# Transposing the exponentials of q with VectorE in 32x32 blocks, from q loaded twice

## The chip, the cores and the metric

The kernel runs on one core of a Trainium2 chip. Time is what one execution takes on the device, in microseconds (us). The core has engines that run beside each other and wait for one another through semaphores: PE (TensorE, the matrix products; PEld is its weight load), DVE (VectorE), ACT (ScalarE), POOL (GpSimd) and SP, which here only issues transfers. Sixteen DMA engines carry out the transfers. SBUF is the on-chip memory with 128 partitions; PSUM holds the results of PE.

## The reference, cut to what matters

The first part is an attention without a score matrix, for 8 batches of 8 heads with 576 tokens of 64 elements. k is normalized over the tokens, q over the 64 elements of a token:

```python
q_s = np.exp(q - np.max(q, axis=-1, keepdims=True))
q_s = q_s / (np.sum(q_s, axis=-1, keepdims=True) + 1e-09)
k_s = np.exp(k - np.max(k, axis=2, keepdims=True))
k_s = k_s / (np.sum(k_s, axis=2, keepdims=True) + 1e-09)
kv = np.einsum('bhsd,bhse->bhde', k_s, v)
x = np.einsum('bhsd,bhde->bhse', q_s, kv)
```

The heads are put side by side, so that a token has 512 elements. The second part picks, in each batch, the 128 tokens of the highest score `x @ w_gate`, runs them through a two-layer network (512 to 1024 with a ReLU, and back) and adds the result times a sigmoid of the score; all other tokens stay as they are:

```python
h = np.maximum(xe @ w1, 0.0)
ye = h @ w2
out[b, top_idx] = x[b, top_idx] + g[:, None] * ye
```

## The kernel before

The attention is cut into 16 units, each of one batch and four heads. Two heads share a tile's 128 partitions, a second pair lies beside it. A unit loads k, v and q (0.59 MB each) into one of three buffers for each of them, so unit u uses buffer u % 3. ACT takes the exponentials of k (`k_exp`) and of q (`q_exp`) and copies v with a column of ones (`v_copy`). PE forms kv for the four heads (`kv_mm`), VectorE normalizes it (`kv_out`), and PE multiplies the exponentials of q with it (`x_mm`), with a column of ones for the sum and one for the score. VectorE divides by the sum (`x_sums`, `x_scale`), and the result is stored (`x_store`).

A matrix product on PE sums over partitions, so q must lie with its 64 elements on partitions. q is loaded with tokens on partitions: a partition of a pair of heads has nine tokens in a row. `q_t` turns it: 18 transposes on PE for a unit (L349, a product with an identity) into PSUM in two parts, of five and of four rows, and a copy of each part back into SBUF. From unit 5 on ACT makes the copy of the first part (L356) and VectorE that of the second (L354); units 0 to 2 use larger transposes (L342).

The dense network of a batch runs two units behind and longer, in pieces that are woven in between: `mlp1` (L544) in odd stages, `mlp2` (L554) in even ones. A stage s of the main loop (L746) holds the attention products of unit s, kv of unit s + 1, the exponentials of q of unit s + 1 and of k of unit s + 2, and one layer of a batch. In odd stages a batch is complete: `score` and `rows` form its row of scores, five compares on VectorE (`ranks`, L446) count for each token how many are above it, and `hits` (L463) marks the ranks. In the next stage `search` finds the tokens' numbers on PE (L473), and POOL gathers the rows (L487). `turn` (L524, copied by L532) transposes the gathered rows for the next layer.

The order of all instructions is written out by hand; every engine runs its own in that order. Transfers of q, k and v and the stores are issued by SP in the order of `queues`: store of unit s (L405), then k and v (L141), then q (L135) of unit s + 3; the first of these loads waits for the last product of `x_mm(s)`. q is loaded in two transfers, of five and of four rows, each over all 128 partitions. A store is two transfers of 64 partitions. k and v are two transfers each of every second partition.

The three q buffers have 18 rows of 64 elements. `ones_f` (for some products at the start), `order_minus_p` (read by L258) and the tiles `hit_f` and `far` (used for batch 0 alone, L499 to L504) are tiles of their own.

Of the kernel before, what the change touches and what calls it, by code (L numbers as in the profile page):

```python
# [8 lines left out]
F32 = mybir.dt.float32  # L9
BF16 = mybir.dt.bfloat16  # L10
I32 = mybir.dt.int32
AF = mybir.ActivationFunctionType
# [5 lines left out]
def kernel(  # L18
# [23 lines left out]
    nc = tc.nc  # L42
    B, H, S, D = q.shape
    DM, F = moe_w1.shape
    P = 128
    R = 5
    N2 = R - 1
    T = R + N2
    RP = N2 * P + P // 2
# [3 lines left out]
    SD = S * D  # L53
# [18 lines left out]
    const = ctx.enter_context(tc.tile_pool(name="const", bufs=1))  # L72
    ld = ctx.enter_context(tc.tile_pool(name="ld", bufs=3))
    at = ctx.enter_context(tc.tile_pool(name="at", bufs=2))
    xp = ctx.enter_context(tc.tile_pool(name="xp", bufs=2))
    md = ctx.enter_context(tc.tile_pool(name="md", bufs=2))
# [3 lines left out]
    def bank(tag, bufs):  # L80
        return ps.tile([P, 512], F32, tag=tag, name=tag, bufs=bufs)

    def pair(tag, bufs=1):
        return ps.tile([P, 2, 512], F32, tag=tag, name=tag, bufs=bufs)
# [4 lines left out]
    def part(i):  # L89
        return slice(64 * i, 64 * i + 64)  # L90
# [7 lines left out]
    NU = len(units)  # L98
# [2 lines left out]

    LD = 3
    FLAT = 0, 1
    RR = 4 * R
    raw = {w: [const.tile([P, 2 * T if w == "q" else RR, D], F32, name=f"{w}{n}") for n in range(LD)] for w in "qkv"}

    def view(t, paired):
        return t.rearrange("p (h r) d -> p h r d", h=4) if paired else t[:, :2 * T].rearrange("p (i r) d -> p i r d", i=2)
# [6 lines left out]
    def load(u, which, after=None, split=False, flat=False):  # L115
        b, qd = units[u]
        for what in which:
            src = {"q": q, "k": k, "v": v}[what]
            first = src[place(b), 4 * qd].offset
            dmas = []  # L120
            if flat:
                t = view(raw[what][u % LD], False)
                if split:
                    for h, queue in enumerate((nc.scalar, nc.sync)):
                        dmas.append(queue.dma_start(out=t[:, h].rearrange("p r d -> p (r d)"),
                                                    in_=bass.AP(tensor=src.tensor, offset=first + 2 * h * SD,
                                                                ap=[[T * D, P], [1, T * D]])))
                else:
                    dmas.append(nc.sync.dma_start(out=t.rearrange("p i r d -> p i (r d)"),  # L129
                                                  in_=bass.AP(tensor=src.tensor, offset=first,  # L130
                                                              ap=[[T * D, P], [2 * SD, 2], [1, T * D]])))
            elif what == "q":
                t = view(raw[what][u % LD], False)
                for r0, r1 in ROWS:
                    dmas.append(nc.sync.dma_start(out=t[:, :, r0:r1].rearrange("p i r d -> p i (r d)"),  # L135
                                                  in_=bass.AP(tensor=src.tensor, offset=first + r0 * D,
                                                              ap=[[T * D, P], [2 * SD, 2], [1, (r1 - r0) * D]])))
            else:
                t = view(raw[what][u % LD], True)
                for n, rows in ((1, N2), (0, R)):  # L140
                    dmas.append(nc.sync.dma_start(out=t[n::2, :, :rows].rearrange("p h r d -> p h (r d)"),  # L141
                                                  in_=bass.AP(tensor=src.tensor, offset=first + n * R * D,
                                                              ap=[[T * D, 64], [SD, 4], [1, rows * D]])))
            if after is not None:
                behind(dmas[0], after)
                after = None
        return dmas[-1]

    ROWS = (0, R), (R, T)
    ctx.enter_context(tc.manual_schedule())  # L150
    load(0, "k", split=True, flat=True)
    load(0, "vq", flat=True)

    def clear(u):
        for what in "kv":
# [5 lines left out]
                                               ap=[[DM, 1], [1, DM]]))  # L161
# [18 lines left out]
    ones_b = const.tile([P, 4 * P], BF16, name="ones_b")  # L180
    nc.vector.memset(ones_b, 1.0)
    w_ps = bank("mm", 2)
    ones_f = const.tile([P, 4 * P], F32, name="ones_f")
    nc.gpsimd.memset(ones_f, 1.0)
    for n in range(WARM):
        nc.tensor.matmul(out=w_ps, lhsT=ones_f[:, :P], rhs=ones_f, start=True, stop=True)
# [20 lines left out]
    for n in range(2):  # L207
        t = const.tile([P, RR, D + 1], F32, name=f"v_ones{n}")
        nc.vector.memset(t[:, :, D:], 1.0)
        v_ones.append(t)  # L210
        t = const.tile([P, 2, C], F32, name=f"kv_w{n}")
        nc.vector.memset(t[:, :, D:D + 1], 1.0)
        kv_w.append(t)
    qrec = const.tile([P, NU, 2, G], F32, name="qrec")
    krec = const.tile([P, NU, 2], F32, name="krec")


    order_minus_p = const.tile([P, RP], F32, name="order_minus_p")
    nc.gpsimd.iota(order_minus_p, pattern=[[1, RP]], base=0, channel_multiplier=-1,
                   allow_small_or_imprecise_dtypes=True)  # L220

# [39 lines left out]
    st = {}  # L261
# [9 lines left out]
    def q_exp(u, c):  # L271
        if c == 0:
            st["qe", u] = at.tile([P, T, 2, D], F32, tag="qe", name="qe")
        r0, r1 = ROWS[c]
        qr = raw["q"][u % LD].rearrange("p (i r) d -> p r i d", i=2)
        nc.scalar.activation(out=st["qe", u][:, r0:r1], in_=qr[:, r0:r1], func=AF.Exp)  # L276

    def v_copy(u, engine=nc.scalar):
# [44 lines left out]
        nc.vector.reduce_sum(out=kw[:, :, D + 1], in_=prod, axis=AX.X)  # L323


    copies = []

    def q_t(u, c, on_vector=False, wide=False, later=False):
# [29 lines left out]
    def x_mm(u, a, wide=False, tag="x"):  # L358

        qT = st["qT", u] if a == 0 else st.pop(("qT", u))  # L360
        x = pair(tag, 2 if tag == "x" else 1)
        kw = kv_w[u % 2]
        for r in range(R):
            for i, c in QUARTERS:
                to = x[part(c), i, r * C:(r + 1) * C]
                if r == N2 and c:
                    last = nc.tensor.matmul(out=to, lhsT=ones_b[part(i), :D], rhs=ones_b[part(i), :C], start=True, stop=True)
                    continue
                if wide and r < N2:
                    if c == 0:  # L370
                        nc.tensor.matmul(out=x[:, i, r * C:(r + 1) * C],
                                         lhsT=qT[part(i), a, r].rearrange("p c t -> p (c t)"), rhs=kw[part(i), a],
                                         start=True, stop=True)
                    continue
                nc.tensor.matmul(out=to, lhsT=qT[part(i), a, r, c], rhs=kw[part(i), a], start=True, stop=True)  # L375
        st["x", u, a] = x[:, :, :R * C].rearrange("p i (r c) -> p i r c", r=R)
        return last

# [113 lines left out]
    def select(b, n, r):  # L492

        k0, m = slots[n]
        if r == 0:
            st["select", n] = bank("mm", 2), md.tile([P, R, P], F32, tag="hit_f", name="hit_f", bufs=1)
        t_ps, hit = st["select", n]
        far = md.tile([P, P], F32, tag="far", name="far")
        nc.scalar.activation(out=far[:, :m], in_=slot_no[:, k0:k0 + m], func=AF.Abs, scale=-1.0,  # L499
                             bias=st["rank", b][:, r:r + 1])  # L500
        nc.scalar.activation(out=hit[:, r, :m], in_=far[:, :m], func=AF.Relu, scale=-1.0, bias=1.0)
        row = xs[b][:, r].rearrange("p n i a d -> p (n i a d)")
        for d in range(KD):
            nc.tensor.matmul(out=t_ps[:, d * m:(d + 1) * m], lhsT=row[:, d * P:(d + 1) * P], rhs=hit[:, r, :m],  # L504
                             start=(r == 0 and d == 0), stop=(r == N2 and d == KD - 1), skip_group_check=True)
        if r == N2:
            turned(b, n, t_ps)
# [74 lines left out]
    def each(step, b, *args):  # L582
        for n in range(n_sl):
            step(b, n, *args)
# [93 lines left out]
    for h in range(2):  # L678
        nc.tensor.matmul(out=g_ps[part(h), :4 * D], lhsT=ones_f[:1, :D],
                         rhs=w_row.rearrange("o (n i x) -> o i n x", i=2, x=2 * D)[:, h], start=True, stop=True)  # L680
# [61 lines left out]
    LAG = 3  # L742
# [3 lines left out]
    for s in range(LAG, NU + LAG):  # L746
# [5 lines left out]
        def pieces(n, to=None):  # L752
            nonlocal f_next
            for _ in range(n if to is None else max(0, to - f_next)):
                each(piece, mlp_b, f_next)
                f_next += 1

        here, follows = s < NU, s + 1 < NU
        ends = s // 2 if here and s % 2 == 1 else None
# [18 lines left out]
        def rows():  # L778
            score_row(ends)

        def ranks(n0=0, n1=R):
            for r in range(n0, n1):
                compare(ends, r)
# [46 lines left out]
        else:  # L830
            if chosen is not None and s not in AFTER:
                pieces(1 if here else 2)
                search()
            if here:
                q_t(s, 0)
                q_t(s, 1, on_vector=s > LAG + 1)
            if follows:
                kv_mm(s + 1)
                kv_out(s + 1)
# [21 lines left out]
            pieces(0, to=2 if follows else 3)  # L861
            if ends is not None:
                rows()
                ranks()
            if s + 2 < NU:
                k_exp(s + 2)
            pieces(0, to=4)
# [4 lines left out]
                number = count_good(good)  # L872
            if ends is not None:
                each(hits, ends)
            pieces(0, to=KF - 1)
            if second and mlp_b + 1 < B:
                each(turn, mlp_b + 1)
# [35 lines left out]
```

## Time and profile before

| | before |
|---|---|
| median of 3 runs | 209.22 us (207.98 to 209.74) |
| time of the profiled execution | 210.15 us |
| its span | 208.4 us |
| transposes of q, units 3 to 15, PE (L349) | 234 in 10.0 us busy |
| copies of them, ACT (L356, 128x640) | 15, mean 692 ns |
| copies of them, DVE (L354, 128x512) | 11, mean 692 ns |
| exponentials of q, ACT (L276) | 32 in 20.1 us busy |
| compares, DVE (L446) | 40 in 32.7 us busy |
| q, issue to landing, median | 6.2 us |
| DMA in all | 46.66 MB, mean 224 GB/s |

The span is the time between the first and the last instruction of the profiled execution. Busy times of an engine are sums over its instructions; those of PE and PEld lie beside each other. The share of an engine's busy time is a mean over a start in which the loads are saturated, a long middle, and a tail with the last batches' network. A DMA share is the mean busy share of the 16 DMA engines; packets of one engine overlap a little, so that it can pass 1.

### The profile page before, as it was taken

Reading aid. Unit: us, or ns where it says so; the run is one execution under the profiler, and the core shown is the slowest. Engines: PE = TensorE matmul, PEld = TensorE weight load, DVE = VectorE, ACT = ScalarE, POOL = GpSimd, SP = SyncE. Lnnn points to the kernel's source line nnn. Section 1 sums busy time; section 2 is a strip of 40 time slices with the busy share of each in tenths; the row PEclk is TensorE's granted clock in tenths of the full one; section 3 lists DMA queues with packets and bytes.
Section 4 is the critical chain, followed back from the end, with each engine's and each line's share of the span. In section 5 each row is a group of like instructions: output and inputs, shape, how many; then the busy total and the mean of one; then the engine's idle time right before and its main releaser. Section 6 shows DMA issues by size and latency. Waiting matters only on the chain.

```text
span 208.4 us, 6943 instructions
## 1 busy us (share of the span) xinstructions
PE 193.6 (93%) x2955; PEld 148.8 (71%) x2955; DVE 119.0 (57%) x361; ACT 92.1 (44%) x135; POOL 32.4 (16%) x93
## 2 busy tenths in 40 slices
PE   7899799798989999999999999999999999999960
PEld 3486789785579848985698759974898579659520
DVE  6668735597167645776378717862776537714010
ACT  3468876574526624545434813672464022111100
POOL 5103000202010101210120104010211012126010
PEclk9999999999999999999999999999999999999995
DMA  6999999999786999995989779895880433131101
GB/s 218 397 307 330 384 360 372 371 381 329 193 296 158 309 327 250 283 279 170 233 282 253 231 175 304 212 314 129 256 247 4 103 110 74 48 101 53 58 5 53
DMA packets 37720, 46.66 MB, mean 224 GB/s; under 512 B 2353, under 2 KB 33073, under 8 KB 37682
## 3 DMA queue, kind: packets, MB, share of 16 engines
q1 hardware_dynamic: 36256, 41.66, 65.2%
q0 software_dynamic: 1280, 4.20, 5.7%
q8 instruction: 25, 0.41, 0.8%
q10 hardware_dynamic: 146, 0.30, 0.5%
q14 instruction: 13, 0.11, 0.2%
HBM read 34.61 MB, written 11.53 MB: 221 GB/s over the span
## 4 chain that ended last, share of the span: by engine, by line
PE 74%; DMA 16%; SPq 3%; issue 1%; ACT 1%; DVE 1%; POOL 0%; POOLq 0%; ACTq 0%
PE mm L544 25%; PE mm L554 25%; DMA k<-in_k_dram 15%; PE x L375 8%; PE kv L310 8%; PE x L349 4%; DMA xr<-out_dram,idx 2%; SPq L141 2%; PE kv L432 2%; PE mm L524 2%; SPq L135 1%; ACT ke L268 1%; PE mm L473 1%; SPq L169 0%; SPq L129 0%
## 5 line engine op out<-in xcount | busy, mean ns | idle before, releaser
L544 PE MATMUL mm<-xT,w 128*128 128x128 f32 x512 | 62.0, 278 | 0.3 <-DVE xT L532 0.3
L544 PEld LDWEIGHTS mm<-xT,w 128*128 128x128 f32 x512 | 58.8, 192 | 2.0 <-ACT xT L532 0.6
L554 PE MATMUL mm<-w,hT 128*128 128x512 f32 x128 | 59.3, 599 | 0.0
L446 DVE SCALAR_TENSOR_TENSOR junk<-srow,s,not_before 128x576 bf16<-128x576 f32 x40 | 32.7, 819 | 9.4 <-ACT srow L438 8.1
L554 PEld LDWEIGHTS mm<-w,hT 128*128 128x128 f32 x128 | 22.6, 190 | 20.6 <-issue 20.1
L567 DVE SCALAR_TENSOR_TENSOR o<-mm,g,xr 128x512 f32<-128x512 f32 x7 | 5.3, 751 | 35.6 <-PE mm L554 35.6
L395 DVE TENSOR_TENSOR xs<-x,qrec 128x640 f32<-128x640 f32 x31 | 24.1, 815 | 0.0
L375 PE MATMUL x<-kv_w,qT 64*64 64x66 f32 x1084 | 21.9, 222 | 1.7 <-issue 1.5
L268 ACT ACTIVATE ke<-k 128x1280 f32<-128x1280 f32 (+1 forms) x16 | 20.0, 1253 | 4.6 <-DMA k<-in_k_dram 4.6
L276 ACT ACTIVATE qe<-q 128x640 f32<-128x640 f32 (+1 forms) x32 | 20.1, 676 | 3.3 <-DMA q<-in_q_dram 3.3
L375 PEld LDWEIGHTS x<-kv_w,qT 64*64 64x64 f32 x1084 | 19.4, 134 | 3.0 <-issue 2.0
L310 PE MATMUL kv<-v_ones,ke 128*64 128x65 f32 x560 | 19.4, 224 | 1.1 <-ACT srow L438 1.1
L310 PEld LDWEIGHTS kv<-v_ones,ke 128*64 128x64 f32 x560 | 17.5, 137 | 2.3 <-ACT srow L438 1.3
L547 ACT ACTIVATE hT<-mm 128x512 f32<-128x512 f32 x16 | 9.6, 597 | 21.5 <-PE mm L544 21.5
L281 ACT COPY v_ones<-v 128x1280 f32<-128x1280 f32 x14 | 17.6, 1257 | 0.7 <-DMA v<-in_v_dram 0.4
L532 ACT COPY xT<-mm 128x512 f32<-128x512 f32 x7 | 4.1, 585 | 30.1 <-PE mm L524 30.1
L487 POOL DMA_INDIRECT xr<-out_dram,idx x8 | 8.3, 1036 | 53.4 <-PE x L349 22.6
L559 POOL DMA_INDIRECT out_dram<-o,idx x7 | 7.0, 996 | 58.9 <-DVE o L567 58.9
L356 ACT COPY qT<-x 128x640 f32<-128x640 f32 (+1 forms) x17 | 11.4, 682 | 9.5 <-PE x L349 8.7
L438 ACT ACTIVATE srow<-kv 128x576 f32<-128x576 f32 x7 | 4.5, 648 | 23.0 <-PE kv L432 23.0
L349 PEld LDWEIGHTS x<-ident,qe 64*128 64x128 f32 x234 | 8.3, 138 | 4.9 <-ACT xT L532 4.5
L354 DVE COPY qT<-x 128x512 f32<-128x512 f32 x11 | 7.6, 692 | 5.8 <-PE x L349 5.8
(115 smaller groups left out, 165.7 us busy)
## 6 DMA issues: line engine op xcount, KB each, us to landing
out_dram<-xs SPq DMA_DIRECT2D x16, 320.0 KB, 3.6
k<-in_k_dram SPq DMA_DIRECT2D x14, 320.0 KB, 5.1
v<-in_v_dram SPq DMA_DIRECT2D x14, 320.0 KB, 6.1
q<-in_q_dram SPq DMA_DIRECT2D x14, 320.0 KB, 6.2
w<-in_moe_w_dram SPq DMA_DIRECT2D x8, 512.0 KB, 7.6
out_dram<-xs SPq DMA_DIRECT2D x16, 256.0 KB, 4.3
k<-in_k_dram SPq DMA_DIRECT2D x14, 256.0 KB, 4.8
v<-in_v_dram SPq DMA_DIRECT2D x14, 256.0 KB, 4.7
```

What stands on the lines that cost most here:

```text
L268: nc.scalar.activation(out=ke, in_=view(raw["k"][u % LD], u not in FLAT), func=AF.Exp)
L276: nc.scalar.activation(out=st["qe", u][:, r0:r1], in_=qr[:, r0:r1], func=AF.Exp)
L281: engine.copy(out=out_v, in_=in_v)
L310: nc.tensor.matmul(out=kv_ps[part(i), a, :D + 1], lhsT=ke[:, 2 * i + a, r], rhs=vo[:, 2 * i + a, r], start=(r == 0), stop=(r == N2))
L349: nc.tensor.transpose(out=src[:, a, r], in_=qe[part(a), r0 + r].rearrange("p i d -> p (i d)"), identity=ident[part(a), part(a)])
L356: nc.scalar.copy(out=to, in_=src)
L375: nc.tensor.matmul(out=to, lhsT=qT[part(i), a, r, c], rhs=kw[part(i), a], start=True, stop=True)
L395: nc.vector.tensor_mul(xs[b][:, :, qd, :, a].rearrange("p r i d -> p i r d"), st.pop(("x", u, a))[:, :, :, :D], rec.to_broadcast([P, 2, R, ...
L446: nc.vector.scalar_tensor_tensor(junk, st["srow", b], st["s", b][:, r:r + 1], not_before[:, r], op0=OP.subtract, op1=OP.is_ge, accum_out=s ...
L544: st["piece"] = nc.tensor.matmul(out=h_ps[:, f % 4 * m:(f % 4 + 1) * m], lhsT=w1[:, d, f * P:(f + 1) * P], rhs=xT[:, d, :m], start=(d == 0 ...
L547: nc.scalar.activation(out=hT[:, f - 3:f + 1, :m], in_=h_ps[:, :4 * m].rearrange("p (f c) -> p f c", f=4), func=AF.Relu)
L554: st["piece"] = nc.tensor.matmul(out=st["y", b, n][:m], lhsT=st["hT", b, n][:, f, :m], rhs=w2[:, f], start=(f == 0), stop=(f == KF - 1))
```

## The change

For units 5 to 15 q is loaded in another form. The 128 partitions are four groups of 32. Groups 0 and 1 hold the first two heads of the unit, groups 2 and 3 the other two; a partition has 18 tokens in a row of each of its two heads. Groups 1 and 3 are loaded with the same tokens, but shifted by 32 elements. So the first 32 of each 64 elements of a row are elements 0 to 31 of a token in one group and 32 to 63 in its neighbour. The other half of each row isn't used. Each group is one transfer of 32 partitions, two heads and rows of 1,120 elements; a unit's q takes four transfers in place of two, and 1.147 MB in place of 0.59 MB.

`q_exp` reads only the used half of each row and writes it densely, 576 elements a partition for each of the two calls. `q_blocks` then transposes blocks of 32x32 on VectorE, one instruction of 128x576 for each of the two heads, from SBUF to SBUF; afterwards the 64 elements of a token lie on 64 partitions. `x_mm` reads its weights from there. The transposes on PE and the copies of `q_t` are gone for these units.

The two calls of `q_blocks` for unit s + 1 stand in stage s: the first after the score row and ahead of the compares in odd stages; the second after the hits there. In even stages both stand after `x_scale` and the gate.

The q buffers grow to 36 rows. `ones_f`, `order_minus_p`, `hit_f` and `far` now lie in the added halves, which the doubled loads use only later. Three memsets on POOL clear the last 32 elements of the added halves.

```diff
-    raw = {w: [const.tile([P, 2 * T if w == "q" else RR, D], F32, name=f"{w}{n}") for n in range(LD)] for w in "qkv"}
+    TWICE = range(5, NU)
+    raw = {w: [const.tile([P, 4 * T if w == "q" else RR, D], F32, name=f"{w}{n}") for n in range(LD)] for w in "qkv"}
+    spare = {n: raw["q"][n].rearrange("p r d -> p (r d)")[:, 2 * T * D:] for n in range(LD)}
...
+            elif what == "q" and u in TWICE:
+                t = raw[what][u % LD].rearrange("p (a n) d -> p a (n d)", a=2)
+                for g in range(4):
+                    dmas.append(nc.sync.dma_start(out=t[32 * g:32 * g + 32, :, :ROW],
+                                                  in_=bass.AP(tensor=src.tensor,
+                                                              offset=first + g // 2 * 2 * SD + g % 2 * D // 2,
+                                                              ap=[[2 * T * D, 32], [SD, 2], [1, ROW]])))
...
+    ROW = 2 * T * D - D // 2
...
-    ones_f = const.tile([P, 4 * P], F32, name="ones_f")
+    ones_f = spare[2][:, :4 * P]
...
+    for n in range(LD):
+        nc.gpsimd.memset(spare[n][:, ROW:], 0.0)
...
-    order_minus_p = const.tile([P, RP], F32, name="order_minus_p")
+    order_minus_p = spare[2][:, 4 * P:4 * P + RP]
...
+        if u in TWICE and u not in FLAT:
+            half = raw["q"][u % LD].rearrange("p (a n) (h s) -> p a n h s", a=2, h=2)[:, c, :, 0]
+            to = st["qe", u].rearrange("p r i d -> p (r i d)").rearrange("p (a n s) -> p a n s", a=2, n=2 * T)
+            nc.scalar.activation(out=to[:, c], in_=half, func=AF.Exp)
+            return
...
+    def q_blocks(u, a):
+        if u not in TWICE:
+            return
+        if a == 0:
+            st["qT", u] = at.tile([P, 2, R, 2, D], F32, tag="qT", name="qT")
+        to = st["qT", u].rearrange("p a r c d -> p a (r c d)")[:, :, :T * D].rearrange("p a (j t e) -> p a e j t", j=T, e=2)
+        qe = st["qe", u].rearrange("p r i d -> p (r i d)").rearrange("p (a e j s) -> p a e j s", a=2, e=2, j=T)
+        nc.vector.transpose(out=to[:, a], in_=qe[:, a])
...
-                nc.tensor.matmul(out=to, lhsT=qT[part(i), a, r, c], rhs=kw[part(i), a], start=True, stop=True)
+                rows = by_token[part(i), a, R * c + r] if u in TWICE and u not in FLAT else qT[part(i), a, r, c]
+                nc.tensor.matmul(out=to, lhsT=rows, rhs=kw[part(i), a], start=True, stop=True)
...
-            st["select", n] = bank("mm", 2), md.tile([P, R, P], F32, tag="hit_f", name="hit_f", bufs=1)
+            st["select", n] = bank("mm", 2), spare[1][:, :R * P].rearrange("p (r t) -> p r t", r=R)
...
-        far = md.tile([P, P], F32, tag="far", name="far")
+        far = spare[1][:, (R + r % 2) * P:(R + r % 2 + 1) * P]
...
-            if here:
+            if here and s not in TWICE:
                 q_t(s, 0)
-                q_t(s, 1, on_vector=s > LAG + 1)
+                q_t(s, 1)
...
+            if follows:
+                q_blocks(s + 1, 0)
+            if ends is not None:
                 ranks()
+            else:
+                q_blocks(s + 1, 1)
...
                 each(hits, ends)
+                q_blocks(s + 1, 1)
```

## The prediction, made before the changed kernel was run

> **What bounds the kernel now.** I read the shares of the engines first, then the chain of work that ended last in order of time, then the engine table by stretches. From 41.6 us to 180 us the chain never leaves TensorE; before that it runs through loads of k.
>
> ```profile
> PE 193.6 (93%) x2955; PEld 148.8 (71%) x2955; DVE 119.0 (57%) x361; ACT 92.1 (44%) x135; POOL 32.4 (16%) x93
> ...
> PE mm L544 25%; PE mm L554 25%; DMA k<-in_k_dram 15%; PE x L375 8%; PE kv L310 8%; PE x L349 4%; DMA xr<-out_dram,idx 2%; SPq L141 2%; PE kv L432 2%; PE mm L524 2%; SPq L135 1%; ACT ke L268 1%; PE mm L473 1%; SPq L169 0%; SPq L129 0%
> ```
>
> One even stage of the chain, from the search to the products of the next turn (start, length, what):
>
> ```profile
> 91.67 0.18 PE mm L473 x5
> 91.86 0.70 PE x L349 x18
> 92.56 1.32 PE kv L310 x40
> 93.88 0.64 PE x L375 x33
> 94.53 0.52 PE x L375 x32
> 95.05 0.15 PE x L375 x5
> 95.20 5.35 PE mm L554 x12
> 100.55 0.44 PE mm L524 x4
> ```
>
> There is no gap: each piece starts where the last one ended. So 0.70 us of transposes (L349) per unit lie on the path with nothing hiding them, and two stages take 22.2 us (90.8 to 113.0).
>
> Now the resource that the change loads more. The stretches of the same two stages (columns: span, length, busy of PE, PEld, DVE, ACT, POOL, clock, DMA share, GB/s), and the saturated stretch before them:
>
> ```profile
> 90.80:101.00 10.20, 10.20 (x159) 6.33 (x158) 4.97 (x17) 4.85 (x7) 1.02 (x1) 1.00 0.73 222
> 101.00:113.00 12.00, 12.00 (x206) 11.04 (x206) 9.02 (x24) 5.96 (x8) 2.33 (x8) 1.00 0.89 249
> ...
> 30.00:41.60 11.60, 10.36 (x260) 9.70 (x256) 6.23 (x22) 7.51 (x12) 1.32 (x7) 1.00 1.07 370
> ```
>
> PE is full, but the DMA engines are busy 10.2 x 0.73 + 12.0 x 0.89 = 18.1 us of 22.2: a share of 0.82, where a full ring shows about 1.06 and 370 GB/s. That is the next bound.
>
> [...]
>
> ```profile
> GB/s 0 0 0 0 0 0 0 135 211 187 187 187 187 187 187 146 170 217 316 298 339 293 123 0 0 0 0 0 0 0 0 0 0 0 0 0 0 0 0 0
> ```
>
> The first store (partitions 0 to 63) holds 187 GB/s; once the second one (64 to 127) is under way the sum is about 310. [...] These are stores; no load of this kind is in the trace. [...]
>
> **The change part by part.**
>
> *Removed, PE:* 18 transposes for each of 11 units (198 of the 234 at L349). 11 x 0.70 = **7.75 us** of the path. The work behind it (kv L310, 1.32) starts that much earlier.
>
> *Removed, copies:* per unit one ACT copy (692 ns) and one VectorE copy (692 ns), 7.6 us each in all. ACT is 44% busy, so this is worth nothing by itself.
>
> *Added, VectorE:* 22 transposes of 128x576 f32. [...] What queues behind it: in odd stages the first transpose stands ahead of the five compares (L446), whose result find (L473) needs at once.
>
> ```profile
> 86.24 0.82 DVE L446 SCALAR_TENSOR_TENSOR junk<-srow,s,not_before 128x576 bf16<-128x576 f32 x1 [1.07 <-ACT srow L438]
> 91.56 0.20 PEld L473 LDWEIGHTS <-hit 128*128 128x128 bf16 x5 [0.72 <-DVE hit L463]
> ```
>
> [...] The second transpose follows the hits and delays the search's reduces by some 0.3 us; the gather behind them (issued at 92.52, landing in 4.8) is needed only at 100.39. It can't gain time, since x (L375) waits for it now as it did for the copies.
>
> *Exponentials:* 2 x 576 elements in place of 640 + 512: the same 1.35 us (735 + 618). x (L375) keeps its count and shape. The three memsets on POOL and the constants that move into the spare halves of q's buffers lie before 8 us, under the first loads: nothing. If the constants' readers had to wait for the load of unit 2 into the same tile, the start would slip by up to 10 us; they touch other columns, so I count none.
>
> *SP queue:* per unit 4 q issues in place of 2: 4 x 0.51 (L135 median) against 1.02, +1 us. After q in the two stages shown the queue is free for 6 us (91.6 to 97.2), so nothing, except in unit 5, whose load (38.8 us) stands ahead of a store and of k of unit 6.
>
> *DMA, the term that decides.* [...] Bounds of its time, against 0.59/0.375 = 1.57 us now (375: between the full stretches, 370 in 30 to 41.6 us, 371 in 72 to 75, 383 in 44 to 47):
> - at full rate 1.147/0.375 = 3.06: +1.5 us;
> - all at the store's 187: 6.1: +4.6 us;
> - the first half at 187 (3.07), the second beside it or at full rate (1.53), as the isolated stores did: 4.6: **+3.0 us**. I take this.
>
> How much fits: the two stages moved 222 x 10.2 + 249 x 12.0 = 5.25 MB, which a full ring takes in 5.25/0.375 = 14.0 us; by their share, 18.1/1.06 = 17.1. With two q's at +3.0: 20.0 to 23.1, middle 21.5. PE would want 22.2 - 1.4 = 20.8. So the DMA becomes the bound by some 0.7 us per pair, 3.6 us over the five pairs from 46 to 157 us. Slack against this: in even stages k's exponential starts at 94.24 and ACT has nothing urgent until the copy of xT at 101.03, some 4 us beyond its 2.5 of work. But k of unit 6 is already waited for (0.35 us, at 50.86), and unit 5's q adds 3.0 ahead of it in a full ring, so 3.4 of the 4 are spent at once. About 3 us of stalls remain. They fall where k is late: ACT stands at k's exponential, hT (L547) or xT (L532) behind it comes late, and PE waits.
>
> **Sum.** -7.75 + 3.0 = -4.7 us. The profiled execution's own time is 210.15 (span 208.4 and 1.75 around it), 0.4% above the median of the runs, 209.22; the difference is applied to the median: **204.5 us**.
>
> **Rivals.**
> [...]
> [...]
> [...]
> - *The change doesn't do what it says:* a false wait on the shared tiles at the start: +10 on whatever else happens. Little chance.
>
> **How the numbers follow.** Forecast 0.35, hidden 0.25, DMA slower 0.30, the last two 0.10. A difference of 1% (2.1 us) is about what a measurement of this kernel can tell from none. Faster by over 1% is below 207.1: all of hidden, three quarters of the forecast (stalls under 5.6) and little else: 0.52. Slower is above 211.3: most of the DMA rival and a part of the last: 0.32. Within 1%: 0.16. The range goes from hidden with a little more freed (200.8) to the DMA rival (219.5). The likeliest case alone runs from 202 to 208.
>
> **What would show it.** L349 at 36 executions; 22 transposes on VectorE near 0.75 us, the compares' idle before them near 0.3. Saturated loads: DMA share near 1 from 46 to 150 us, q landing later than its 6.2 us, ACT waiting for k (L268) by some us in all. [...]

## The result, and the profile after

| | before | after |
|---|---|---|
| median of 4 runs each, same chip | 208.87 us | 225.33 us (223.85 to 228.89) |
| ratio, 95% interval | | 1.0765 (1.0683 to 1.0847), slower |
| time of the profiled execution, its span | 210.15, 208.4 us | 224.95, 222.9 us |

A ratio here compares undisturbed runs with undisturbed runs of the kernel before on the same chip, so it can differ a little from the quotient of two medians. The kernel before had medians of 208.87 to 212.36 us on the chips used, so kernels are compared by their ratios; a point below is a hundredth of such a ratio, some 2.1 us.

The changed file is some 29 lines longer at this place: the products of x are now L404, kv L328, find L502, the gather L516, the turn of the gathered rows L553 and its copy L561, the two layers L573 and L583, the compares L475, k's exponential L281, the copy of v L299, the VectorE transposes L351.

From the page of the kernel after: engines, granted clock and DMA share in 40 slices, the main DMA ring (q1, the queue of the transfers that SP issues), the chain that ended last by engine and by line, and two groups.

```profile
PE 194.5 (87%) x2755; PEld 146.0 (65%) x2757; DVE 126.6 (57%) x372; ACT 85.8 (39%) x124; POOL 32.6 (15%) x96
...
PEclk9999999996966999999957999999999999999995
DMA  6999999999994999999999799999999051531101
...
q1 hardware_dynamic: 33792, 47.79, 74.8%
...
PE 41%; DMA 37%; DVE 9%; SPq 4%; issue 3%; ACT 2%; POOL 0%; POOLq 0%; DVEq 0%; ACTq 0%
...
L553 PE MATMUL mm<-ident,xr 128*128 128x128 f32 x28 | 4.8, 300 | 13.2 <-DMA xr<-out_dram,idx 13.2
...
L351 DVE STREAM_TRANSPOSE qT<-qe 128x576 f32<-128x576 f32 x22 | 16.3, 763 | 0.0
```

Three readings. The chain, which stayed on PE from 41.6 us before, is now 37% DMA, most of it the gather (`xr<-out_dram,idx`, 21% of the span by line). The ring q1 was busy for 74.8% of 222.9 us = 166.7 us, against 65.2% of 208.4 = 135.9: 30.9 us more for 11 units, **2.8 us for each q**. The records of the single packets in the traces agree: those of 4,480 bytes are the changed q's alone, and they took 4.85 us per unit over the 16 engines, which leaves 113.3 us for the rest of the ring, or 2.05 for each q before if the rest is the same. And PE was busy for longer than before (194.5 against 193.6) with 200 instructions fewer: its clock fell in five slices (digits 5 to 7) in the midst of the work, where before it was 9 in all slices but the last.

Where the time went shows when the span is cut at each find (L473 before, L502 after), one cut per two stages. Before (columns: span, length, busy of PE, PEld, DVE, ACT, POOL, granted clock, DMA share, GB/s):

```profile
47.88:69.31 21.43, 19.91 (x303) 15.41 (x303) 12.58 (x37) 11.02 (x15) 2.51 (x8) 1.00 0.81 242
69.31:91.59 22.28, 22.28 (x363) 17.45 (x363) 14.16 (x40) 10.92 (x15) 3.34 (x9) 1.00 0.97 288
91.59:113.87 22.28, 22.28 (x364) 17.45 (x364) 14.07 (x40) 10.81 (x15) 3.35 (x9) 1.00 0.81 237
```

After:

```profile
47.16:78.82 31.66, 24.21 (x285) 17.61 (x285) 14.11 (x40) 10.54 (x14) 2.50 (x8) 0.84 0.94 244
78.82:100.95 22.13, 21.05 (x327) 16.09 (x327) 15.42 (x43) 9.81 (x13) 3.34 (x9) 1.00 1.05 301
100.95:129.34 28.39, 23.41 (x327) 17.65 (x327) 15.47 (x43) 9.87 (x13) 3.35 (x9) 0.88 0.99 245
129.34:151.33 21.99, 21.06 (x328) 16.10 (x328) 15.43 (x43) 9.61 (x13) 3.35 (x9) 1.00 1.00 287
151.33:174.58 23.25, 21.05 (x327) 16.09 (x327) 15.43 (x43) 9.73 (x13) 3.35 (x9) 1.00 0.93 250
```

PE's own work for a pair of stages fell as meant, from 22.28 to 21.05 us. But no pair runs at that length, and two are 10.2 and 6.1 us longer than the same pairs before. In those two PE is also busy for longer than its instructions need at the full clock: the clock is 0.84 and 0.88. The five pairs together take 127.4 us, against 110.5 before: the 16.9 us between them are more than the 14.5 between the two spans.

The long pair from 100.95 in the chain of waits, in order of time (start, length, what):

```profile
101.04 0.18 PE mm L502 x5
101.22 1.34 PE kv L328 x40
...
104.06 0.14 DVE qrec L418
104.20 0.03 issue
104.23 9.82 DMA xr<-out_dram,idx
114.06 0.14 issue
114.19 1.09 PE mm L553 x4
115.28 1.71 PE mm L583 x2
```

The rows' numbers were ready at 101.66 (L507, by the timeline), but the gather was issued only at 104.23 and then took 9.8 us to land; the turn (L553) stood for 5.0 us. Before, the same gather was issued at 92.52, 0.28 us after its index, and landed in 4.8; the turn began at 100.39, so it had 3 us to spare. The gather reads rows of `out` that stores have just written. Of the store issued at 94.56, the first transfer took 8.0 us to land, against 3.8 and 3.9 for two stores before; the landing of its second transfer isn't in the trace. The chain names a VectorE instruction as what released the gather at 104.23; as that is no input of a gather, I take the landing of this store as the more likely cause, which is not shown. A late store isn't needed for a late gather: those at 79.81 and 130.85 were issued 0.3 and 0.8 us after their index and still took 8.2 and 7.5 us. The median landing of the stores rose from 3.6 and 4.3 us to 6.7 and 7.4, of the gathers from 4.8 to 7.9.

All waits of PE from 40 to 190 us (total, times, longest):

```profile
PE mm L553 <- DMA xr<-out_dram,idx: 12.9, 5, 5.0
PE x L404 <- issue: 3.7, 2, 2.0
PE kv L328 <- ACT srow L467: 0.4, 1, 0.4
```

Before, the gather cost PE 0.2 us there, and everything else 2.6. The line with "issue" is two stops of 1.8 and 2.0 us within x in the first long pair, for which the profile shows no releaser; their cause stays open.

### The profile page after: what moved, and what is told of

The parts are those of the page before. It is cut to its first block, busy times and chain, and to the rows that moved or that the text cites. A ratio compares the mean times of both kernels' runs of the same rounds, so it can differ in the third digit from the quotient of the medians.

```text
span 222.9 us, 6578 instructions
## 1 busy us (share of the span) xinstructions
PE 194.5 (87%) x2755; PEld 146.0 (65%) x2757; DVE 126.6 (57%) x372; ACT 85.8 (39%) x124; POOL 32.6 (15%) x96
## 3 DMA queue, kind: packets, MB, share of 16 engines
q1 hardware_dynamic: 33792, 47.79, 74.8%
## 4 chain that ended last, share of the span: by engine, by line
PE 41%; DMA 37%; DVE 9%; SPq 4%; issue 3%; ACT 2%; POOL 0%; POOLq 0%; DVEq 0%; ACTq 0%
DMA xr<-out_dram,idx 21%; PE mm L573 17%; DMA k<-in_k_dram 16%; PE mm L583 10%; DVE junk L475 6%; PE kv L328 6%; PE x L404 4%; PE mm L553 2%; SPq L151 2%; PE kv L461 1%; ACT srow L467 1%; DVE hit L492 1%; SPq L180 1%; DVE qT L351 1%; ACT ke L281 1%
## 5 line engine op out<-in xcount | busy, mean ns | idle before, releaser
L573 PE MATMUL mm<-xT,w 128*128 128x128 f32 x512 | 63.3, 282 | 0.3 <-DVE xT L561 0.3
L583 PE MATMUL mm<-w,hT 128*128 128x512 f32 x128 | 62.7, 628 | 0.0
L573 PEld LDWEIGHTS mm<-xT,w 128*128 128x128 f32 x512 | 60.0, 195 | 2.7 <-ACT xT L561 1.3
L583 PEld LDWEIGHTS mm<-w,hT 128*128 128x128 f32 x128 | 23.5, 198 | 21.7 <-issue 20.9
L475 DVE SCALAR_TENSOR_TENSOR junk<-srow,s,not_before 128x576 bf16<-128x576 f32 x40 | 32.7, 819 | 6.5 <-ACT srow L467 5.2
L404 PE MATMUL x<-kv_w,qT 64*64 64x66 f32 x1084 | 22.1, 223 | 4.5 <-issue 3.7
L424 DVE TENSOR_TENSOR xs<-x,qrec 128x640 f32<-128x640 f32 x31 | 24.1, 816 | 0.0
L404 PEld LDWEIGHTS x<-kv_w,qT 64*64 64x64 f32 x1084 | 19.5, 134 | 6.1 <-issue 4.2
L328 PEld LDWEIGHTS kv<-v_ones,ke 128*64 128x64 f32 x560 | 19.3, 149 | 6.3 <-ACT xT L561 3.8
L281 ACT ACTIVATE ke<-k 128x1280 f32<-128x1280 f32 (+1 forms) x16 | 20.1, 1254 | 8.6 <-DMA k<-in_k_dram 8.6
L328 PE MATMUL kv<-v_ones,ke 128*64 128x65 f32 x560 | 21.3, 236 | 0.4 <-ACT srow L467 0.4
L299 ACT COPY v_ones<-v 128x1280 f32<-128x1280 f32 x14 | 17.6, 1256 | 7.8 <-DMA v<-in_v_dram 7.1
L561 ACT COPY xT<-mm 128x512 f32<-128x512 f32 x7 | 4.1, 585 | 34.8 <-PE mm L553 34.8
L516 POOL DMA_INDIRECT xr<-out_dram,idx x8 | 8.3, 1035 | 59.8 <-DVE no L508 23.6
L553 PE MATMUL mm<-ident,xr 128*128 128x128 f32 x28 | 4.8, 300 | 13.2 <-DMA xr<-out_dram,idx 13.2
L351 DVE STREAM_TRANSPOSE qT<-qe 128x576 f32<-128x576 f32 x22 | 16.3, 763 | 0.0
L553 PEld LDWEIGHTS mm<-ident,xr 128*128 128x128 f32 x28 | 3.3, 151 | 18.5 <-issue 18.5
L337 DVE RECIPROCAL krec<-kv 128x2 f32<-128x2 f32 x16 | 2.7, 169 | 21.2 <-PE kv L328 20.0
```

The costliest lines, as they stand in the source:

```text
L281: nc.scalar.activation(out=ke, in_=view(raw["k"][u % LD], u not in FLAT), func=AF.Exp)
L299: engine.copy(out=out_v, in_=in_v)
L328: nc.tensor.matmul(out=kv_ps[part(i), a, :D + 1], lhsT=ke[:, 2 * i + a, r], rhs=vo[:, 2 * i + a, r], start=(r == 0), stop=(r == N2))
L351: nc.vector.transpose(out=to[:, a], in_=qe[:, a])
L404: nc.tensor.matmul(out=to, lhsT=rows, rhs=kw[part(i), a], start=True, stop=True)
L424: nc.vector.tensor_mul(xs[b][:, :, qd, :, a].rearrange("p r i d -> p i r d"), st.pop(("x", u, a))[:, :, :, :D], rec.to_broadcast([P, 2, R, ...
```

## The experiments

My theory after this result: the compute side gave what was forecast, and the loads took it back twice, by filling the ring (k and v late) and by delaying the store and the gather behind it. The rivals: the loss comes from the transposes on VectorE or the shared tiles; or from the bytes as such and not from the 32 partitions; or from the gather alone.

**Small loads, the change's compute.** q is loaded as before; each of the two calls of the exponential reads one half of every row.

```diff
-            elif what == "q" and u in TWICE:
+            elif what == "q" and u in ():
...
-            half = raw["q"][u % LD].rearrange("p (a n) (h s) -> p a n h s", a=2, h=2)[:, c, :, 0]
+            half = raw["q"][u % LD][:, :2 * T].rearrange("p n (h s) -> p n h s", h=2)[:, :, c]
```

> Everything of the change but the loads: q of units 5 to 15 comes in the two 128-partition transfers of before (0.59 MB), and the exponentials read 32 of every 64 elements of those rows, so q's elements stand in other places than the reference's. If the loads are the whole loss, the transposes' gain of 7.75 us shows alone: 200 to 203 us. If VectorE's 22 transposes of 763 ns hold PE (through compares, hits and find), it stays above 207.

Measured: 202.27 us, ratio 0.9631 (0.9554 to 0.9708). Its pairs, cut at the finds as above:

```profile
90.56:111.43 20.87, 20.87 (x328) 16.18 (x328) 15.33 (x43) 9.64 (x13) 3.35 (x9) 1.00 0.87 251
111.43:132.31 20.88, 20.88 (x328) 16.19 (x328) 15.41 (x43) 9.53 (x13) 3.35 (x9) 1.00 0.87 254
```

PE has no gap in these two, and the five pairs together take 103.0 us. The compute side is worth 0.0369 x 208.87 = 7.7 us; the loads therefore cost 225.33 - 201.2 = **24.1 us**, and transposes on VectorE are no part of the loss.

**As many bytes over all partitions.** 1.147 MB of q in two transfers over 128 partitions, rows of 4,480 bytes.

```diff
-                for g in range(4):
-                    dmas.append(nc.sync.dma_start(out=t[32 * g:32 * g + 32, :, :ROW],
...
+                for a in range(2):
+                    dmas.append(nc.sync.dma_start(out=t[:, a, :ROW],
+                                                  in_=bass.AP(tensor=src.tensor, offset=first + a * SD,
+                                                              ap=[[T * D, P], [1, ROW]])))
```

> The 1.147 MB per unit of the change, but in two transfers over all 128 partitions with the same rows of 4,480 bytes; the rows read are others than the reference's. [...] If the bytes alone are the cost, it stays at 218 to 226.

Measured: 205.71 us, ratio 0.9820 (0.9738 to 0.9902). The ring worked 145.5 us, 0.87 more per q than before, and moved 296 GB/s at a share of 0.90 from 39 to 165 us, where the changed kernel moved 271 at a share of 1.00. By the packet records a packet of q, 4,480 bytes in both kernels, took 192 ns here and 303 in the changed one. So the doubled bytes cost 1.9 points of the 11.3 between 0.9631 and 1.0765; the other 9.4 come from the form, 32 partitions a transfer. (There are also two transfers here in place of four; that their number matters little is seen below, with eight.)

**Another order of the groups.** 0, 2, 1, 3: neighbours in the queue go to different halves of the partitions.

```diff
-                for g in range(4):
+                for g in (0, 2, 1, 3):
```

> [...] If each transfer of 32 partitions is slow by itself, or the order of two halves doesn't matter: 223 to 228.

Measured: 218.64 us, ratio 1.0413 (1.0330 to 1.0496), 3.5 points better than the change; the ring worked 162.1 us, 2.4 per q, at 283 GB/s. But PE still waited 13.1 us for the gathers, which landed in 7.7.

**Eight transfers.** In that order, and each head by itself.

```diff
-                for g in (0, 2, 1, 3):
-                    dmas.append(nc.sync.dma_start(out=t[32 * g:32 * g + 32, :, :ROW],
+                for a, g in ((a, g) for a in range(2) for g in (0, 2, 1, 3)):
+                    dmas.append(nc.sync.dma_start(out=t[32 * g:32 * g + 32, a, :ROW],
```

> [...]

Measured: 221.37 us, ratio 1.0427 (1.0375 to 1.0479), the same as with four. Between these two it doesn't matter how finely the halves alternate, nor how many transfers carry q.

**Two queues.** Groups 2 and 3 issued from ACT.

```diff
-                for g in range(4):
-                    dmas.append(nc.sync.dma_start(out=t[32 * g:32 * g + 32, :, :ROW],
+                for g in (0, 2, 1, 3):
+                    queue = nc.scalar if g // 2 else nc.sync
+                    dmas.append(queue.dma_start(out=t[32 * g:32 * g + 32, :, :ROW],
```

> [...]

Measured: 235.71 us, ratio 1.1098 (1.1033 to 1.1162), the worst of all. The gathers landed in 4.6 us, but k and v came late (waits of ACT in its profile):

```profile
ACT ke L282 <- DMA k<-in_k_dram: 22.2, 6, 7.0
ACT v_ones L300 <- DMA v<-in_v_dram: 20.2, 8, 4.0
```

Why k and v came later with q on a second ring was not shown; the cause stays open.

**No wait for the gather.** The turn reads a constant tile, so that nothing on PE waits for gathered rows; the gathers are still issued.

```diff
-            nc.tensor.transpose(out=t_ps[:, d * m:(d + 1) * m], in_=xr[:m, d * P:(d + 1) * P],
+            nc.tensor.transpose(out=t_ps[:, d * m:(d + 1) * m], in_=w2[:m, 0, d * P:(d + 1) * P],
```

> PE's transposes of the gathered rows read rows of w2 in place of them (so the network runs on other rows; the sum at the end still waits for the gathered ones). If the chain store, gather, turn is what costs, with the ring itself only slow and not the bound, 12.9 us of PE's waits go and the time falls to 208 to 214 us. If the DMA engines' work is the bound (share 1.0 from 39 to 165 us), the wait moves to k, v or q and the time stays at 220 to 226.

Measured: 216.07 us, ratio 1.0300 (1.0199 to 1.0401): 4.65 points, 9.7 us, come back, so neither of the two expectations holds alone. Four of its five pairs:

```profile
69.90:94.63 24.73, 21.28 (x328) 16.25 (x327) 15.87 (x43) 9.90 (x13) 3.36 (x9) 1.00 1.04 283
94.63:119.44 24.81, 22.55 (x327) 17.55 (x328) 15.75 (x42) 9.79 (x13) 3.37 (x9) 0.93 1.03 281
119.44:142.79 23.35, 21.22 (x326) 16.25 (x327) 15.63 (x42) 9.90 (x13) 3.35 (x9) 1.00 1.01 279
142.79:166.16 23.37, 20.94 (x327) 16.18 (x328) 15.16 (x42) 9.99 (x13) 3.35 (x9) 1.00 0.97 264
```

and the waits that took the gather's place:

```profile
ACT ke L281 <- DMA k<-in_k_dram: 23.6, 11, 3.5
...
ACT v_ones L299 <- DMA v<-in_v_dram: 18.2, 10, 3.5
```

The long pairs are gone. The first pair takes 21.7 us and the other four 23.4 to 24.8: this is what the ring alone allows with the change's loads. In the changed kernel ACT waited only 8.6 us for k and 7.1 for v; that PE, standing at the turn for 12.9 us, gave the ring time to catch up is my reading and was not shown. The five pairs (48.23 to 166.16) take 117.9 us. With 103.0 for those of the small loads and 127.4 for the change, the loss divides: **14.9 us for the ring, 9.5 more with the gather's wait.**

The 9.5 us are not all time spent waiting for rows. In the changed kernel the two long pairs take 10.0 and 3.6 us more than the same pairs here, the other three 4.1 less, and the first long pair also holds the two unexplained stops and PE's lower clock. A higher clock isn't needed for the gain, though: two of the runs without the wait had a mean granted clock of 0.960, as high as the changed kernel's 0.951 to 0.960, and took 215.92 and 216.12 us.

**No v.** From unit 6 on v isn't loaded, 0.59 MB less per unit; the products use old values of v.

```diff
+            if what == "v" and u >= 6:
+                continue
```

> The changed kernel without the loads of v from unit 6 on (v of earlier units is used again), so 1.6 us of full-rate work per unit less in the ring. If the DMA engines' work per stage is the bound, about 10 x 1.6 = 16 us come back: 206 to 211 us. [...]

Measured: 218.48 us, median of four runs, against 212.36 before, but they lie at 214.35, 218.29, 218.67 and 220.00. Something comes back, but the scatter allows no reading of how much, and no ratio is given; this run decides nothing.

**No v and no wait for the gather.** Both edits together.

> The changed kernel with both taken away: PE's transposes don't wait for the gathered rows (they read rows of w2), and v isn't loaded from unit 6 on. If the loss is made of these two, the late gathers and the work of the ring that holds back k and v, nearly nothing is left: 202 to 206 us where before takes 209. If each of the two hid the other's stall and a third (VectorE, the clock of PE after a stall) is left: 208 to 214.

Measured: 209.82 us against 212.03 before, ratio 0.9786 (0.9715 to 0.9857). Taken away together, the ring's work and the gather's wait give back 9.8 of the 11.3 points of loss. (A unit's v is 0.59 MB, about what the change added, 0.56, so this is a measure of the ring's relief and not of q itself.)

**No wait for the gather, other order.** The edits of two runs above together.

> PE's transposes don't wait for the gathered rows, and q's groups come in the order 0, 2, 1, 3. If the order saves ring time alone, its 6.7 us come on top of the 9 of the gather: 208 to 211 us. If the order helped through earlier gathers, no more than the missing wait alone: 214 to 217.

Measured: 211.98 us, ratio 0.9950 (0.9916 to 0.9984). From 1.0765, less 3.5 points for the order and 4.65 for the gather, would be 0.995: the two gains add, so the order saves ring time and doesn't work through the gather's wait.

**Odd units only, even units only.** Both with the order 0, 2, 1, 3. (First line odd, second even.)

```diff
-    TWICE = range(5, NU)
+    TWICE = range(7, NU, 2)
+    TWICE = range(6, NU, 2)
```

> Only units 7, 9, 11, 13, 15 take the change, with groups in the order 0, 2, 1, 3. Their q is issued at the end of even stages and is through before the next store that a gather needs. Five units' transposes are worth 3.5 us. If the loss comes from the chain store, gather, turn in a full ring, these loads don't meet it: 204 to 208 us against 209. If the DMA engines' whole work per two stages decides, one q of +2.4 us in 22 fits as well: about the same. If every doubled q costs PE what it did in the changed kernel (2.1 us each), 211 to 215.

> The same for units 6, 8, 10, 12, 14, whose q is issued beside the gather of an even stage. Same bytes and same transposes saved as with the odd units. If the gather's chain matters, each gather is some 2 us later than its 3 us of slack allow only in part: 209 to 213 us, slower than the odd units by 3 or more. If only the DMA engines' whole work matters, the two are equal within 1 us.

Measured: odd 214.61 us, ratio 1.0088 (1.0049 to 1.0126); even 220.66, 1.0256 (1.0179 to 1.0334). Five units each, 1.7 points or 3.6 us apart, as expected if the gather's chain matters; but odd units, which don't meet it, gain nothing either, against the 204 to 208 us expected of them. With even units the gathers landed in 8.0 us and PE waited 6.8 us for them; with odd units in 4.4, and 0.4 (in a profiled execution of 217.59 us, above its median). The timeline of the even case shows the likely reason (a q of the new form, then the gather):

```profile
95.95 1.96 SPq L138 DMA_DIRECT2D q<-in_q_dram  x4
...
98.08 1.03 POOL L516 DMA_INDIRECT xr<-out_dram,idx  x1 [6.89 <-DVE no L508]
```

In even stages s the q of unit s + 3 is odd, in odd stages even. The even one is issued just before the search is done, and the gather starts behind it, here at 95.95 and 98.08; with odd units it is the old, smaller q that stands there. In the changed kernel the same stands at 101.13, ahead of the gather at 104.23. With odd units 4.1 us of "issue" ahead of x (L404) remain, for which the profile shows no releaser: open.

**Three units only.** Units 13 to 15.

```diff
-    TWICE = range(5, NU)
+    TWICE = range(13, NU)
```

> The change for units 13 to 15 alone. Three units' transposes are worth 2.1 us. If a q of 2.8 us more fits where the ring is idle a fifth of the time (share 0.78 to 0.89), 206 to 208 us; if each such q makes one gather late by itself, as the changed kernel's first ones did, 210 to 214.

Measured: 213.56 us, ratio 1.0045 (1.0005 to 1.0086). Even three units gain nothing: in its profile (an execution of 215.98 us) one wait of 2.9 us for a gather takes more than the 3 x 0.70 us of transposes.

**No unit changed.** The changed file with an empty range: shared tiles, memsets and larger buffers remain.

```diff
-    TWICE = range(5, NU)
+    TWICE = range(NU, NU)
```

> The code of the change with no unit taking it: q loaded once and transposed by PE, both copies of q's transposes on ACT, and the four constants in the spare halves of q's buffers. If these side changes are worth nothing, within 0.5% of before; if they cost something, that part of the loss with five and three units is theirs and not the loads'.

Measured: 211.62 us, ratio 0.9995 (0.9970 to 1.0020). The shared tiles cost nothing.

**The loads alone.** The change's loads with the transposes on PE and the copies of before, which read q in the wrong places.

```diff
-        if u in TWICE and u not in FLAT:
+        if u in ():
...
-            if here and s not in TWICE:
+            if here:
```

> The loads of the change with the transposes and copies of before (PE, ACT, VectorE); q's elements stand in other places than the reference's. If the DMA engines set the pace, PE's transposes fit into the waits and the time is that of the changed kernel, 223 to 229 us. If the two parts add up on the path, the loads cost 225.3 - 202.3 = 23 us on top of 209: 230 to 234.

Measured: 230.93 us against 212.26 before, ratio 1.0889 (1.0820 to 1.0958), 1.2 points or 2.6 us above the change. The two intervals overlap a little, so this is rough: with the ring as the bound, taking the transposes off PE is worth some 2.6 us, a third of the 7.7 it is worth without these loads.

**q in an idle ring.** No unit changed; at the end, one unit's q is loaded three times: in the change's form, in the order 0, 2, 1, 3, and over all partitions.

```diff
+            for order in ((0, 1, 2, 3), (0, 2, 1, 3)):
+                for g in order:
+                    nc.sync.dma_start(out=t[32 * g:32 * g + 32, :, :ROW],
...
+            for a in range(2):
+                nc.sync.dma_start(out=t[:, a, :ROW],
```

> The kernel with q loaded once and transposed by PE, and at the end, where the ring is idle, three loads of a unit's 1.147 MB one after the other, each waiting for the one before: the four transfers in the order of groups 0 to 3, the same in the order 0, 2, 1, 3, and two transfers over all partitions. [...] If partitions don't matter, all three are alike.

A single execution, 215.93 us. The 40 slices of 178:186 us, which hold the end of a store (until 180), then the first set and the start of the second:

```profile
DMA  8998999899999997989998998999998999998996
GB/s 189 184 215 174 184 205 159 143 205 271 302 369 267 264 300 284 403 269 246 291 224 179 246 224 224 269 336 269 224 246 202 224 269 179 202 202 202 291 358 134
DMA packets 967, 1.93 MB, mean 241 GB/s; under 512 B 99, under 2 KB 668, under 8 KB 966
```

and of 193:201, with the third set:

```profile
DMA  0000000000098979977279999999999995410010
GB/s 22 22 0 0 0 0 0 0 0 0 0 224 112 179 134 202 179 112 134 90 246 381 442 461 412 390 403 410 494 373 416 377 426 202 179 67 0 0 41 0
```

From 182 to 186, with nearly nothing but q, 32-partition transfers move 235 GB/s at a share of 1.01. The third set starts at 137 GB/s at a share of 0.85 (195 to 197), and only then moves 404 at 0.99 (197 to 199.5, stores of the gathered rows among it). So it took 5.1 us from its first packet to its last, as long as the first set; why it started slowly is open. As a timing of one q this run doesn't separate the forms; that is shown by the run in the full ring above (192 against 303 ns a packet). The second set took 8.2 us, with gathers among it, so that the orders can't be compared here.

## Why the prediction was wrong

The forecast was 204.5 us (range 200.8 to 219.5); measured were 225.33.

- **Removed from PE, -7.75 us: right.** 7.7 us with the small loads. "PE would want" 20.8 per pair: 20.87.
- **VectorE's transposes near 0.75 us, at no cost: right.** No run before the change shows the 0.75; it was an estimate of mine, and the transposes took 763 ns. VectorE had idled 1.07 us ahead of the first compare shown, and after the change, in four of the five stages concerned, it idled 0.38 to 0.39 there, where 0.3 was expected.
- **Copies, exponentials, SP and the shared tiles at nothing: right** so far as the runs separate them: 0.9995 with no unit changed, and no gap on PE with the small loads.
- **q costs +3.0 us of DMA time: right in size.** The ring worked 2.8 us more per unit. The bound of +4.6 was too high. The argument behind the +3.0, a first half at 187 GB/s and a second beside it or at full rate, was not shown for loads: its rates are those of the last pair of stores before, alone in the ring (174:181). And the 371 GB/s of 72 to 75 held q as well, which was issued from 67.92 us on and landed in 6.2. From 75 to 76.5, with q through, the trace of before has 319 GB/s at a share of 0.94.
- **"About 3 us of stalls remain. They fall where k is late": this step failed.** The loads cost 24.1 us in place of 3. Two parts of it were wrong.

*The size for the ring.* I had 20.0 us by bytes and 23.1 by share for a pair of stages, and took "middle 21.5". The runs stood at the upper end and above: with the gather's wait taken away, the pairs took a mean of 117.9/5 = 23.6 us. The lower bound assumed that the rest of the traffic (k, v, stores, gathers) moved at 375 GB/s. It didn't even before the change: the three pairs of before shown above, 237 to 288 GB/s at shares of 0.81 to 0.97, come to 293 to 299 GB/s at a full share. With 295 in place of 375 the sum is 5.25/0.295 + 6.0 = 23.8, where 23.6 was measured. Not the q term was too small, but the base beneath it. So the stall from late k and v was 14.9 us over five pairs, and not 3; that alone turns -4.7 into a loss (the 1.0300 of the run without the gather's wait).

*The place.* I followed k through the full ring, but not the other transfers in it. The prediction names the gather once, for the 0.3 us that VectorE delays it, with "issued at 92.52, landing in 4.8" and "needed only at 100.39". That landing was measured in a ring that was not full (share 0.73). Its slack was 3 us; in the full ring the store ahead of it took some 3 us longer, and so did the gather itself. With both late, PE waited 12.9 us, and the five pairs took 9.5 us beyond the ring's part. In the two pairs with the longest waits PE's clock was lower too (0.84 and 0.88), which the prediction left out; how much of the 9.5 that is, stays open.

Of the other cases, *hidden* (0.25) fell with the pairs of 22 to 32 us. *DMA slower* (0.30) had the right sign and the right resource, but its end of the range, 219.5, was passed by 5.8 us, though a q cost 2.8 us more and not the bound of 4.6. Of the last two (0.10), VectorE as the new bound fell with the small loads and the false wait on the shared tiles with the "no unit" run.

Of the signs of saturated loads named ahead, the share came to 1.00, at 271 GB/s (39 to 165 us), and q landed in a median of 9.0 us in place of 6.2, but k's waits came to only 8.6 us. The wait for the gather stood in their place; with it taken away they were 23.6.

No version that computes all of the result beat the kernel before: the best ones with the doubled q, three units (1.0045) and odd units (1.0088), are no gain.

## What to carry to other kernels

When a change fills a queue that had room left, list every transfer in it that something waits for, with its own slack, and price each at the landing time of a full ring: here stores and gathers took 3 us longer, and a chain of two of them with 3 us to spare held PE for 12.9 us. Where a resource's remaining room comes out differently by bytes and by busy share, take the share: here the DMA engines were busy all the time (1.00) at 271 GB/s, and nine tenths of it (0.90) at 296. And try the cheap half alone: the compute side was worth 7.7 us, if only its operand could be had without the 32-partition loads.

## What the runs showed of the hardware

- q's packets of 4,480 bytes took 303 ns each in transfers of 32 partitions (changed kernel, DMA share 1.00) and 192 ns in transfers over all partitions (share 0.90). Over 16 engines that is 237 and 373 GB/s (worked out from these).
- Alternating the halves of the partitions gave 3.3% of the whole time in the full ring (1.0413 against 1.0765), and cut each q's ring time from 2.8 to 2.4 us beyond that of before, well short of the 0.87 of the same bytes over all partitions. The ring as a whole moved 283 GB/s in place of 271. For stores the trace of before shows more: the last pair, 64 partitions each and alone in the ring (174:181), went from 187 GB/s to some 310 once its second half was under way.
- PE's granted clock fell to 0.84 and 0.88 in the pairs with waits of 3.7 and 5.0 us for the gather, and stayed at 1.00 in those with waits of 0.9 to 2.2. By the pairs' busy times this cost 24.21 - 18.71 (as many instructions with the small loads) and 23.41 - 21.05, together some 7.9 us of PE's work, an estimate. The four runs of the change had mean granted clocks of 0.951 to 0.960, those with the small loads 0.981 to 0.993. That the waits lower the clock was not tested apart, and in other runs the clock fell at other places, as in a pair (0.93) of the run without the gather's wait.
